# Rotary attention and a dense mixture of experts on one core: shorter rope tables, joined tail loads, a new order for the first batch's pairs, two subtractions moved to VectorE and four sums moved to GpSimd

## The chip, the cores and the metric

The kernel runs on one core of a Trainium2 chip. The metric is the device time of one execution in microseconds (us). Before the change it is 558.88 us, the median of three runs that lie between 558.83 and 558.90.

A core has five engines that run their own instruction streams and wait for each other on semaphores: TensorE (PE, matrix products; PEld is its loading of weights), VectorE (DVE), ScalarE (ACT), GpSimd (POOL) and SyncE (SP, which here only starts DMA transfers). [...]

## The reference

Attention with rotary embedding for q, k and v of shape 2 x 8 x 576 x 64, and a dense mixture of four experts over its output (1152 tokens of 512 values):

```python
def rotate(x):                       # cos, sin: 576 x 32, by position
    x1, x2 = x[..., :half], x[..., half:]
    return concat([x1 * cos - x2 * sin, x1 * sin + x2 * cos], -1)
scores = matmul(rotate(q), rotate(k).T) / sqrt(64)
attn = softmax(scores)               # exp(scores - max), over the sum + 1e-9
x = matmul(attn, v)                  # transposed to 1152 tokens x 512
p = domain_probs / (domain_probs.sum(-1) + 1e-9)
for e in range(4):                   # w1: 512 x 1024, w2: 1024 x 512
    h = maximum(x @ w1[e], 0)
    out += p[:, e:e+1] * (h @ w2[e])
```

## The kernel before

Most operands are split: a float32 value becomes a high part in the format fp32r and a low part, the difference between the value and its high part (`split`, L139 to L149). A product is then three matmuls: high by high, low by high, high by low. The high part is a copy, the low part a subtraction that reads two tiles from SBUF.

**First batch (0 to about 96 us).** Its eight heads are taken as four pairs (`Pair`). A pair's 576 positions are four blocks of 128 and a tail of 64; the tails of the pair's two heads share one block. Nine units `u` of work (four blocks for each head, then both tails) each go through: scores on PE (L365), row maximum on DVE (`max`, L376, tile `mx`), exponential on ACT (L387, tile `e`), transposes on PE (`turn_e`, L403, tile `pp`), a copy of these out of PSUM on DVE or ACT (`keep_e`, L430 to L437, tile `pt`), and the product with v (`values_of_four`, L446 to L455, one burst for each head). Then the division by the row sums, and the split of the pair's output into `xH` and `xL`, the operands of the experts: `xf`, 128x512, is the main part (`out_high` L562, `out_low` L566) and `xt`, 128x64, the tail (`tail_high` L587, `tail_low` L590 to L592). The low parts go to the engine that `spare_engine` (L594) names.

The order of issue is set by plan times: `place` (L597) puts each step of a unit on a heap (`Agenda`, L1036) at the pair's start plus the unit's number plus an entry of a table (`ALONE` for the first batch, `BESIDE` for the second), and the heap is emptied in the order of these numbers. The numbers are no times of the chip. One table serves all four pairs.

**Startup.** The rope tables come in one DMA on ACT's queue (L1138), laid out as `[128, 2, 5, 64]`: cosine, then sine with its sign, 64 values for each position, and ACT copies four blocks of each for the second head (L1145). q and k of a pair come in a DMA for the blocks (L181) and two of 64x64 for the tails, one for each head (L187). DVE rotates the first pair's k (L203, L207, L211, then its split), POOL its q and, behind that, q and k of the second pair; PE transposes them (`tpk`, `tpq`, L312).

**Second batch and first 512 tokens of the experts (about 96 to 343 us).** The experts' first layer (`ph`, L793 to L795), its split (`hH`, `hL`) and second layer (`po`, L768 to L770) run between the steps of the second batch's attention. The weights are split as they arrive: ACT copies the high part (L680, `wh`, 128x1024), POOL subtracts (L681, `wl`).

**Last 640 tokens (about 343 to 552 us).** `Moe1` computes the first layer with seven products over halves, for which `Weights.sum` (L692) forms four sums of weight blocks (`sf`, L701), then their split (`sh` on ACT, `sl` on POOL). For the first weight block of expert 0 the sums are POOL's, otherwise DVE's. DVE also adds the products up (L971) and makes `hL` (L982).

Of the kernel before, what the change touches and what calls it, by code (L numbers as in the profile page):

```python
# [22 lines left out]

ALONE = dict(
    scores=-0.216, max=-0.086, exp=0.449, turn_e=1.843, keep_e=1.923, turn_x=1.854, keep_x=2.839, values=3.902,
    keep_values=3.939, keep_values_2=4.037, tail_turn=1.866, copy_e=2.785, tail_turn_x=1.883, copy_x=2.045,
    inverse=1.86, spread=2.789, rows=3.299, divide=3.371, out_high=6.829, out_low=7.765, tail_rows=2.632,
    keep_tail_rows=3.895, tail_values=2.929, tail_divide=4.52, tail_high=4.659, tail_low=5.033,
)
BY_VECTOR = (0, 2)  # L30
BESIDE = dict(
# [4 lines left out]
    tail_low=2.554,  # L36
)

TURNS = [
    dict(  # L40
        k0=(5.275, 5.496), k1=(5.861, 6.017), q0=(7.136, 7.195), q1=(9.095, 9.116), k_tails=(5.379, 5.571),
        q_tails=(9.309, 9.652), swap=7.117,
    ),
    dict(
        k0=(3.155, 3.369), k1=(3.874, 3.89), q0=(6.063, 6.216), q1=(7.829, 8.028), tails=(5.059, 5.169),
        swap=5.239,
    ),
    dict(
        k0=(2.921, 3.395), k1=(4.09, 4.369), q0=(6.714, 6.914), q1=(7.075, 7.485), tails=(5.006, 5.12),
        swap=8.171,  # L50
    ),
]
# [10 lines left out]
def kernel(  # L63
# [75 lines left out]
    def split(eng_h, eng_l, src, hi, lo):  # L139
# [9 lines left out]
        eng_l.tensor_tensor(out=lo, in0=src, in1=f32(hi), op=ALU.subtract)  # L149


    class Pair:
# [12 lines left out]
        def load(self, s, queue=nc.sync, heads=((0, 2),)):  # L165
# [14 lines left out]
            for i, (a, z) in enumerate(heads):  # L180
                queue.dma_start(  # L181
                    out=x[:, a:z, 0:NR, :], in_=hs[a:z, 0:SM, :].rearrange("h (p r) d -> p h r d", r=NR)
                )
                if i:
                    continue
                for j in range(2):
                    queue.dma_start(out=x[j * ST : (j + 1) * ST, 0, NR, :], in_=hs[j, SM:S, :])  # L187
            self.raw[s] = x

        def rotate(self, which, eng, a=0, z=NC, pool=None):  # L190
# [11 lines left out]
            hl = self.hl[which][:, a:z]  # L202
            eng.tensor_tensor(out=t1, in0=x, in1=tabs[:, 0, a:z], op=ALU.mult)  # L203
            yield
            for lo, hi in ((0, D // 2), (D // 2, D)):
                o = D // 2 - lo
                eng.tensor_tensor(  # L207
                    out=t2[:, :, lo:hi], in0=x[:, :, o : o + D // 2], in1=tabs[:, 1, a:z, lo:hi], op=ALU.mult
                )
# [6 lines left out]
        def rotate_whole(self, which, eng):  # L216
# [6 lines left out]
            x = self.raw[which].rearrange("p h r d -> p (h r) d")[:, 0:NC]  # L223
            eng.tensor_tensor(out=t1, in0=x, in1=tabs[:, 0], op=ALU.mult)
            yield
            for lo, hi in ((0, D // 2), (D // 2, D)):
                o = D // 2 - lo
                eng.tensor_tensor(
                    out=t2[:, :, lo:hi], in0=x[:, :, o : o + D // 2], in1=tabs[:, 1, :, lo:hi], op=ALU.mult
                )  # L230
# [363 lines left out]
        def spare_engine(self):  # L594
            return nc.vector if (self.b, self.hp) == (B - 1, NP - 1) else nc.gpsimd

        def place(self, u, t, step, o):  # L597
# [8 lines left out]
            if u == TAIL:  # L606
                at("tail_turn", self.turn_e, u)
                at("tail_turn_x", self.turn_x, u)
                for key in (
                    "copy_e", "copy_x", "inverse", "spread", "rows", "divide", "out_high", "out_low", "tail_rows", "keep_tail_rows",  # L610
                    "tail_values", "tail_divide", "tail_high", "tail_low",
                ):
# [3 lines left out]
            if self.plain:
                at("keep_e", self.keep_e, u, nc.vector if u % NR in BY_VECTOR else nc.scalar)
                if u % 2:
                    at("turn_x", self.turn_x, u)
                    at("keep_x", self.keep_x, u)  # L620
                if u % NR == NR - 1:
                    j = u // NR
                    at("values", self.values_of_four, j)
                    at("keep_values", self.keep_values, j, 0, nc.vector)
                    at("keep_values_2", self.keep_values, j, 1, nc.scalar)
                return
            at("high", self.high, u)
# [7 lines left out]
    class Weights:  # L635
# [501 lines left out]
    apart = ((0, 1), (1, 2))  # L1137
    nc.scalar.dma_start(out=tabs[:, :, 0:NS], in_=rope)  # L1138
# [5 lines left out]
    for x in range(2):  # L1144
        nc.scalar.activation(out=tabs[:, x, NS:], in_=tabs[:, x, 0:NR], func=AF.Copy)  # L1145
    pr.rotate_now("k", nc.vector, 0, NS)
# [48 lines left out]
    for hp, pr in enumerate(first):  # L1195
        n = hp * U
        for u in range(U):
            pr.place(u, n + u, 1, ALONE)
        if hp + 1 < NP:
# [7 lines left out]
            plan.at(n + t["swap"], nx.swap)  # L1207
    load_qk(2.6, first[2])
    load_v(U + 5.8, first[2])
    load_qk(U + 0.05, first[3])  # L1210
    load_v(2 * U + 5.8, first[3])
    load_qk(2 * U + 0.4, second[0])
    load_v(3 * U + 9.3, second[0])
    for t in (6.5, 21.2, 30.2):
        plan.at(t, wts.load)
    for t in (30, 33):
        plan.at(t, later(wts.split))
    end = NP * U + 8.5
    for i in range(int(2 * end) - 1):
# [73 lines left out]
def _rope_tables(S, D):  # L1293
# [40 lines left out]
```

## Time and profile before

| | before |
|---|---|
| median of the runs | 558.88 us |
| profiled execution, its own time | 558.97 us |
| its span, first to last instruction | 557.2 us |
| PE busy, share of the span | 532.4 us, 96% |
| DVE | 317.5 us, 57% |
| ACT | 273.9 us, 49% |
| POOL | 318.3 us, 57% |
| mean granted TensorE clock, share of full speed | 0.998 |

The busy shares are means over stages that differ. PE is the only engine near its limit, so the time can be read as PE's busy time plus the stretches in which PE stands: 557.2 - 532.4 = 24.8 us, of which 4.7 us come after its last matmul. In a listing of waits, "A <- B" says that A's engine stood until B was done.

### The profile page before, as it was taken

What the parts mean: (1) busy time and instruction counts of PE and PEld (TensorE: products, weight loads), DVE (VectorE), ACT (ScalarE), POOL (GpSimd) and SP (SyncE); (2) the same over time, 40 slices, a digit from 0 to 9 for tenths busy, and PEclk for the clock granted to TensorE, in tenths of its full rate; (3) what the DMA queues carried; (4) which work ended last, traced back from release to release, by engine and by line L of the source; (5) the groups of instructions that cost most, each with busy time, mean ns of one, the idle gap of its engine ahead of it and who ended that gap; (6) DMA issues with size and microseconds to landing.
All of it is one profiled execution on the core that took longest, in us unless ns stands there. A gap on an engine that the chain in (4) does not pass through costs nothing.

```text
span 557.2 us, 8532 instructions
## 1 busy us (share of the span) xinstructions
PE 532.4 (96%) x3189; PEld 459.9 (83%) x3189; DVE 317.5 (57%) x605; ACT 273.9 (49%) x556; POOL 318.3 (57%) x238
## 2 busy tenths in 40 slices
PE   3899989999999999999999999999999999999996
PEld 2677777788888888888788878988998899889985
DVE  6578675444465435554365427894777477657602
ACT  4667666663565546564556554352443234315300
POOL 7999914659334933483453497478555653565400
PEclk9999999999999999999999999999999999999999
DMA  5525303453235222522252215431232223222102
GB/s 153 137 64 142 80 1 101 124 167 103 76 74 153 75 77 73 155 77 76 49 137 75 76 41 177 162 114 38 77 113 77 76 68 120 78 63 91 38 1 94
DMA packets 48731, 51.16 MB, mean 92 GB/s; under 512 B 15538, under 2 KB 38322, under 8 KB 48690
## 3 DMA queue, kind: packets, MB, share of 16 engines
q1 hardware_dynamic: 47890, 49.87, 30.3%
q10 hardware_dynamic: 800, 0.75, 0.5%
q8 instruction: 25, 0.41, 0.3%
q14 instruction: 16, 0.13, 0.1%
HBM read 43.34 MB, written 2.36 MB: 82 GB/s over the span
## 4 chain that ended last, share of the span: by engine, by line
PE 77%; ACT 7%; DVE 6%; POOL 5%; issue 1%; SPq 1%; DMA 1%; ACTq 0%; DVEq 0%; POOLq 0%
PE po L1030 6%; PE po L1029 6%; PE po L1028 6%; PE sc L365 6%; PE p L942 6%; PE p L940 6%; PE p L941 5%; PE ph L794 4%; PE ph L795 4%; PE po L770 4%; PE po L768 4%; PE ph L793 4%; PE po L769 4%; PE pp L403 4%; PE x L455 3%; ACT e L387 2%
## 5 line engine op out<-in xcount | busy, mean ns | idle before, releaser
L681 POOL TENSOR_TENSOR wl<-wr,wh 128x1024 fp32r<-128x1024 f32 x64 | 154.0, 2411 | 145.5 <-ACT wh L680 145.5
L680 ACT ACTIVATE wh<-wr 128x1024 fp32r<-128x1024 f32 x64 | 67.2, 1052 | 21.8 <-issue 11.0
L376 DVE TENSOR_REDUCE mx<-sc 128x1 f32<-128x576 f32 x72 | 54.3, 754 | 33.3 <-PE sc L365 31.3
L149 POOL TENSOR_TENSOR sl<-sf,sh 128x1024 fp32r<-128x1024 f32 x16 | 38.5, 2408 | 43.4 <-ACT sh L142 43.4
L387 ACT ACTIVATE e<-sc,mx 128x576 f32<-128x576 f32 x72 | 53.4, 742 | 19.2 <-DVE mx L376 18.9
L1030 PE MATMUL po<-wh,hL 128*128 128x512 f32 x160 | 62.3, 389 | 0.0
L1029 PE MATMUL po<-wl,hH 128*128 128x512 f32 x160 | 62.3, 389 | 0.0
L1028 PE MATMUL po<-wh,hH 128*128 128x512 f32 x160 | 62.3, 389 | 0.0
L768 PE MATMUL po<-wh,hH 128*128 128x512 f32 x128 | 51.6, 403 | 0.0
L793 PE MATMUL ph<-xH,wh 128*128 128x512 f32 x128 | 51.1, 399 | 0.0
L794 PE MATMUL ph<-xL,wh 128*128 128x512 f32 x128 | 50.1, 391 | 0.8 <-POOL xL L566 0.8
L795 PE MATMUL ph<-xH,wl 128*128 128x512 f32 x128 | 50.1, 392 | 0.0
L770 PE MATMUL po<-wh,hL 128*128 128x512 f32 x128 | 50.1, 392 | 0.0
L769 PE MATMUL po<-wl,hH 128*128 128x512 f32 x128 | 49.9, 390 | 0.0
L980 ACT ACTIVATE hH<-p 128x320 fp32r<-128x320 f32 x64 | 26.0, 435 | 38.8 <-DVE p L971 38.8
L403 PE MATMUL pp<-ident,e 128*128 128x128 f32 x288 | 43.8, 275 | 1.2 <-ACT e L387 0.8
L754 DVE SCALAR_TENSOR_TENSOR hL<-ph,hH 128x512 fp32r<-128x512 f32 x32 | 22.2, 692 | 39.8 <-ACT hH L753 39.6
L701 DVE TENSOR_TENSOR sf<-wr 128x256 f32<-128x256 f32 x30 | 33.1, 1141 | 17.0 <-DMA wr<-in_moe_w_dram 17.0
L142 ACT ACTIVATE sh<-sf 128x1024 fp32r<-128x1024 f32 x16 | 17.0, 1060 | 51.1 <-DVE sf L701 51.1
L403 PEld LDWEIGHTS pp<-ident,e 128*128 128x128 f32 x288 | 34.3, 140 | 7.6 <-ACT e L387 2.2
L982 DVE SCALAR_TENSOR_TENSOR hL<-p,hH 128x320 fp32r<-128x320 f32 x64 | 30.9, 486 | 14.8 <-ACT hH L980 14.5
L803 DVE SCALAR_TENSOR_TENSOR acc<-po,probs,acc 128x512 f32<-128x512 f32 x27 | 18.6, 748 | 33.0 <-PE po L1030 32.9
(221 smaller groups left out, 1307.8 us busy)
## 6 DMA issues: line engine op xcount, KB each, us to landing
wr<-in_moe_w_dram SPq DMA_DIRECT2D x68, 512.0 KB, 3.5
k2T<-kT SPq DMA_DIRECT2D x14, 320.0 KB, 4.4
rawv<-in_v_dram SPq DMA_DIRECT2D x16, 128.0 KB, 3.1
out_dram<-acc SPq DMA_DIRECT2D x8, 256.0 KB, 2.8
rawk<-in_k_dram SPq DMA_DIRECT2D x7, 256.0 KB, 3.8
rawq<-in_q_dram SPq DMA_DIRECT2D x7, 256.0 KB, 3.0
rawv<-in_v_dram SPq DMA_DIRECT2D x16, 32.0 KB, 2.3
tabs<-in_rope_dram ACTq DMA_DIRECT2D x1, 320.0 KB, 3.5
```

The costliest lines, as they stand in the source:

```text
L403: nc.tensor.transpose(pp[:, c * P : (c + 1) * P], self.e[u][:, c * P : (c + 1) * P], ident)
L680: nc.scalar.activation(out=wh, in_=raw, func=AF.Copy)
L681: low = lambda: nc.gpsimd.tensor_tensor(out=wl, in0=raw, in1=f32(wh), op=ALU.subtract)
L768: nc.tensor.matmul(po[t], lhsT=sH, rhs=wH, start=(f == 0), stop=False)
L769: nc.tensor.matmul(po[t], lhsT=sH, rhs=wL, start=False, stop=False)
L770: nc.tensor.matmul(po[t], lhsT=sL, rhs=wH, start=False, stop=(f == NF - 1))
L793: nc.tensor.matmul(o, lhsT=wH[:, kt], rhs=xh, start=(kt == 0), stop=False)
L794: nc.tensor.matmul(o, lhsT=wH[:, kt], rhs=xl, start=False, stop=False)
L795: nc.tensor.matmul(o, lhsT=wL[:, kt], rhs=xh, start=False, stop=(kt == KT1 - 1))
L1028: nc.tensor.matmul(po[t], lhsT=sH, rhs=wH, start=(f == 0), stop=False)
L1029: nc.tensor.matmul(po[t], lhsT=sH, rhs=wL, start=False, stop=False)
L1030: nc.tensor.matmul(po[t], lhsT=sL, rhs=wH, start=False, stop=(f == NF - 1))
```

## The change

It has seven parts.

1. The tables are 96 values for each position (cosine once, minus sine, sine) instead of 128. Cosine is broadcast over both halves (`times_cos`). The DMA is 128x480 values (240 KB) instead of 128x2x320 (320 KB), and ACT's copy is one of 128x384 instead of two of 128x256.
2. The two tail DMAs of each k and q load become one with a source of [2, 64, 64] and 128 partitions as its destination. At the start SP issues the second pair's k and q ahead of all v loads.
3. Three tables (`PAIRS`) replace `ALONE`: for the first pair, the two middle ones and the last; each unit has its own entries, and they also choose DVE or ACT for the copies.
4. The value burst is placed in three parts (blocks 0 and 1, 2 and 3, the rest).
5. `spare_engine` gives DVE the low parts of the last pair of both batches; before, that was so for the second batch alone.
6. In the second batch's last pair the four transposes of the tail's exponentials go ahead of the last group of value products (`BESIDE_VALUES`).
7. The four sums of the last weight block of expert 0 go to POOL, and their split is in two halves of 128x512. The sums are formed in the order 0, 1, 2, 3.

```diff
-    tabs = const.tile([P, 2, 2 * NR + 1, D], F32, name="tabs")
+    tabs = const.tile([P, NC, 3 * D // 2], F32, name="tabs")
...
+    def times_cos(eng, out, x, a, z):
+        cos = tabs[:, a:z, 0 : D // 2].unsqueeze(2).to_broadcast([P, z - a, 2, D // 2])
+        halves = (y.rearrange("p n (two d) -> p n two d", two=2) for y in (out, x))
+        eng.tensor_tensor(out=next(halves), in0=next(halves), in1=cos, op=ALU.mult)
...
-                for j in range(2):
-                    queue.dma_start(out=x[j * ST : (j + 1) * ST, 0, NR, :], in_=hs[j, SM:S, :])
+                queue.dma_start(out=x[:, 0, NR, :], in_=hs[:, SM:S, :])
...
-            eng.tensor_tensor(out=t1, in0=x, in1=tabs[:, 0, a:z], op=ALU.mult)
+            times_cos(eng, t1, x, a, z)
...
         def spare_engine(self):
-            return nc.vector if (self.b, self.hp) == (B - 1, NP - 1) else nc.gpsimd
+            return nc.vector if self.hp == NP - 1 else nc.gpsimd
...
+        def place_alone(self, u, n, o):
             def at(key, f, *args):
-                plan.at(t + step * o[key], lambda: f(*args))
+                plan.at(n + o[f"{key}{u}"], lambda: f(*args))
...
+                for key, chunks in (("values_a", (0, 2)), ("values_b", (2, 4)), ("values_c", (4, 5))):
+                    at(key, self.values_of_four, j, chunks)
...
+            ends = not e and fb in (0, NF // FB - 1)
             for o, p, q, op in (
-                (0, a21, a22, ALU.add), (2, a11, a21, ALU.subtract), (1, x[:, 0], a11, ALU.subtract),
+                (0, a21, a22, ALU.add), (1, x[:, 0], a11, ALU.subtract), (2, a11, a21, ALU.subtract),
                 (3, a12, x[:, 1], ALU.subtract),
             ):
-                (nc.vector if e or fb else nc.gpsimd).tensor_tensor(out=x[:, o], in0=p, in1=q, op=op)
+                (nc.gpsimd if ends else nc.vector).tensor_tensor(out=x[:, o], in0=p, in1=q, op=op)
...
-            if e or fb:
+            if ends and fb:
+                for i in (0, 2):
+                    split(nc.scalar, nc.gpsimd, *(y[:, i : i + 2] for y in (x, sh, sl)))
+            elif e or fb:
                 split(nc.scalar, nc.gpsimd, x, sh, sl)
...
-    pr.load("v")
-    for s in "kqv":
+    for s in "kq":
         nx.load(s)
+    for x in (pr, nx):
+        x.load("v")
...
-            pr.place(u, n + u, 1, ALONE)
+            pr.place_alone(u, n, PAIRS[0 if not hp else 2 if hp == NP - 1 else 1])
...
+            late = BESIDE_VALUES if hp == NP - 1 and u == TAIL - 1 else {}
+            pr.place(u, n + step * (u + 2), step, dict(when, **late))
```

Three places show what this does to the order. Line numbers are those of the respective kernel, and the numbers at the names' ends are instances.

The first is the end of the first batch's last pair (`xf_3`, `xt_3`) on POOL; `wl_0_0_2` and `wl_0_0_3` are the low parts of expert 0's next weight blocks, `vs` the split of the second batch's first v. Before:

```order
77 L144 TENSOR_SCALAR vs_0_1265<-rawv_0_1260 128x10x64
78 L149 TENSOR_TENSOR vs_0_1265<-rawv_0_1260,vs_0_1265 128x10x64
79 L592 TENSOR_TENSOR xL_76<-xt_3_1313,xH_74 128x64
80 L566 TENSOR_TENSOR xL_75<-xf_3_1215,xH_73 128x512
81 L681 TENSOR_TENSOR wl_0_0_2_1319<-wr_0_0_2_1141,wh_0_0_2_1318 128x1024
82 L681 TENSOR_TENSOR wl_0_0_3_1331<-wr_0_0_3_1316,wh_0_0_3_1330 128x1024
```

And after, first POOL, then DVE at the same place (`kT_0` belongs to the second batch's first pair):

```order
76 L635 TENSOR_TENSOR xL_75<-xf_2_956,xH_73 128x512
77 L204 TENSOR_SCALAR vs_0_1268<-rawv_0_1263 128x10x64
78 L209 TENSOR_TENSOR vs_0_1268<-rawv_0_1263,vs_0_1268 128x10x64
79 L767 TENSOR_TENSOR wl_0_0_2_1308<-wr_0_0_2_1126,wh_0_0_2_1307 128x1024
80 L767 TENSOR_TENSOR wl_0_0_3_1320<-wr_0_0_3_1305,wh_0_0_3_1319 128x1024
```

```order
115 L538 COPY xf_3_1204<-x_122 64x256
116 L629 TENSOR_TENSOR xf_3_1204<-xf_3_1204,pr_3_1296 128x512
117 L652 TENSOR_TENSOR xt_3_1302<-x_122,xt_3_1302 64x64 x2
118 L661 TENSOR_TENSOR xL_76<-xt_3_1302,xH_74 128x64
119 L635 TENSOR_TENSOR xL_75<-xf_3_1204,xH_73 128x512
120 L366 SCALAR_TENSOR_TENSOR kT_0_1329<-tpk_0_1322,kT_0_1329 64x512 x2
```

The two subtractions have left POOL, so its two `wl` follow `vs` directly, and stand on DVE between the divisions and `kT_0`. ACT's order there is unchanged: the copy `wh_0_0_2`, then `xH` from `xt_3`, `xH` from `xf_3`, then `wh_0_0_3`.

The second is the value burst of the first batch's second pair on PE (`x_122 <- pt_1_0`). Before, then after:

```order
83 L312 MATMUL tpq_2_695<-identr,hlq_20_370 128x128 x4
84 L365 MATMUL sc_1_7_705<-kT_1_380,qT_1_449 128x288 x2
85 L365 MATMUL sc_1_7_705<-k2T_1_441,qT_1_449 128x288 x2
86 L403 MATMUL pp_1_5_710<-ident,e_1_4_643 128x128 x4
87 L475 MATMUL x_121<-ident,e_1_4_643 128x128
88 L455 MATMUL x_122<-pt_1_0_548,rawv_1_158 64x256 x8
```

```order
83 L379 MATMUL tpq_2_686<-identr,hlq_20_363 128x128 x4
84 L524 MATMUL x_122<-pt_1_0_538,rawv_1_154 64x256 x4
85 L432 MATMUL sc_1_7_699<-kT_1_372,qT_1_442 128x288 x2
86 L432 MATMUL sc_1_7_699<-k2T_1_434,qT_1_442 128x288 x2
87 L470 MATMUL pp_1_5_704<-ident,e_1_4_629 128x128 x4
88 L544 MATMUL x_121<-ident,e_1_4_629 128x128
89 L524 MATMUL x_122<-pt_1_0_538,rawv_1_154 64x256 x4
```

Half of the rows of the burst's first product now stand ahead of the scores of unit 7. The third pair has the same exchange.

The third is DVE while the last 640 tokens go through the first hidden blocks of expert 0; `sf_3` are the four sums of part 7. Before:

```order
324 L982 SCALAR_TENSOR_TENSOR hL_0_1_3958<-p_3_3831,hH_0_1_3957 128x320
325 L701 TENSOR_TENSOR sf_3_3980<-wr_0_2_3_3796 128x256
326 L982 SCALAR_TENSOR_TENSOR hL_0_0_3888<-p_0_3970,hH_0_0_3887 128x320
327 L701 TENSOR_TENSOR sf_3_3980<-wr_0_2_3_3796 128x256
328 L701 TENSOR_TENSOR sf_3_3980<-sf_3_3980,wr_0_2_3_3796 128x256
329 L701 TENSOR_TENSOR sf_3_3980<-wr_0_2_3_3796,sf_3_3980 128x256
330 L971 TENSOR_TENSOR u_1_3999<-p_1_3992,p_0_1_3850 128x320
```

After, on POOL:

```order
178 L209 TENSOR_TENSOR sl_2_3912<-sf_2_3906,sh_2_3911 128x1024
179 L788 TENSOR_TENSOR sf_3_3963<-wr_0_2_3_3779 128x256
180 L788 TENSOR_TENSOR sf_3_3963<-sf_3_3963,wr_0_2_3_3779 128x256
181 L788 TENSOR_TENSOR sf_3_3963<-wr_0_2_3_3779 128x256
182 L788 TENSOR_TENSOR sf_3_3963<-wr_0_2_3_3779,sf_3_3963 128x256
183 L209 TENSOR_TENSOR sl_3_3970<-sf_3_3963,sh_3_3969 128x512 x2
```

The four sums now stand behind `sl_2` on POOL, and DVE goes from `hL_0_0` directly to `u_1`. For experts 1 to 3 they stay on DVE, with the second and third exchanged.

## Rows read from the trace of the kernel before

**Rows 1.** Waits of PE: what waited <- for what, total us, times, longest.

```profile
PE tlq L335 <- POOL xL L149: 1.4, 1, 1.4
...
PE tpq L312 <- POOL hlq L149: 0.9, 1, 0.9
PE ph L794 <- POOL xL L566: 0.8, 1, 0.8
...
PE x L507 <- DVE ptX L486: 0.7, 1, 0.7
PE p L940 <- DVE hL L982: 0.6, 1, 0.6
```

**Rows 2.** Timeline 96 to 104 us: start, duration, engine, line, [idle before].

```profile
96.35 1.06 ACT L680 ACTIVATE wh<-wr 128x1024 fp32r<-128x1024 f32 x1
97.32 0.24 ACT L588 ACTIVATE xH<-xt 128x64 fp32r<-128x64 f32 x1
...
97.99 1.04 ACT L680 ACTIVATE wh<-wr 128x1024 fp32r<-128x1024 f32 x1
98.16 1.27 POOL L566 TENSOR_TENSOR xL<-xf,xH 128x512 fp32r<-128x512 f32 x1 [0.20 <-ACT xH L563]
99.39 4.75 POOL L681 TENSOR_TENSOR wl<-wr,wh 128x1024 fp32r<-128x1024 f32 x2
...
99.48 0.50 PE L794 MATMUL ph<-xL,wh 128*128 128x512 f32 x1 [0.85 <-POOL xL L566]
```

**Rows 3.** Timeline 362 to 385 us, two-input subtractions on POOL and DVE.

```profile
370.67 7.32 POOL L681 TENSOR_TENSOR wl<-wr,wh 128x1024 fp32r<-128x1024 f32 x3 [1.65 <-ACT wh L680]
374.08 4.20 DVE L701 TENSOR_TENSOR sf<-wr 128x256 f32<-128x256 f32 x2
```

**Rows 4.** Stretches: length, PE, PEld, DVE, ACT, POOL busy, PEclk, DMA share, GB/s.

```profile
552.50:553.00 0.50, 0.02 (x1) 0.00 (x0) 0.50 (x2) 0.00 (x0) 0.00 (x0) 1.00 1.00 377
...
555.00:555.50 0.50, 0.00 (x0) 0.00 (x0) 0.00 (x0) 0.00 (x0) 0.00 (x0) 0.50 0.90 279
```

**Rows 5.** Timeline of PE, the first scores and the same form later.

```profile
11.57 0.81 PE L365 MATMUL sc<-kT,qT 128*128 128x288 f32 x2
...
16.27 0.49 PE L365 MATMUL sc<-kT,qT 128*128 128x288 f32 x2
```

**Rows 6.** DMA issues: target <- source, queue, count, KB each, us to landing.

```profile
tabs<-in_rope_dram ACTq DMA_DIRECT2D x1, 320.0 KB, 3.5
...
rawk<-in_k_dram SPq DMA_DIRECT2D x16, 16.0 KB, 3.1
```

**Rows 7.** Timeline of POOL at its first rotation and its last at startup.

```profile
4.88 0.45 POOL L203 TENSOR_TENSOR t1q<-rawq,tabs 128x128 f32<-128x128 f32 x1 [1.91 <-DMA rawq<-in_q_dram]
...
27.25 1.40 POOL L149 TENSOR_TENSOR hlq<-t1q,hlq 128x576 fp32r<-128x576 f32 x1
```

**Rows 8.** Page part 3, DMA queues: packets, MB, share of 16 engines' span.

```profile
q1 hardware_dynamic: 47890, 49.87, 30.3%
```

**Rows 9.** Timelines at 45 us and 80 to 82 us, PE and DVE.

```profile
45.29 0.54 PE L365 MATMUL sc<-kT,qT 128*128 128x288 f32 x2 [0.18 <-ACT e L387]
...
80.60 0.76 DVE L376 TENSOR_REDUCE mx<-sc 128x1 f32<-128x576 f32 x1
...
...
81.72 0.53 PE L365 MATMUL sc<-kT,qT 128*128 128x288 f32 x2 [1.40 <-ACT e L387]
```

**Rows 10.** Timeline of PE at 333 us, the tail's four transposes.

```profile
332.91 0.60 PE L403 MATMUL pp<-ident,e 128*128 128x128 f32 x4
```

**Rows 11.** Timelines at 344 us and 359 to 365 us, the sums and their split.

```profile
344.36 0.87 POOL L701 TENSOR_TENSOR sf<-wr,sf 128x256 f32<-128x256 f32 x1
...
359.79 0.41 DVE L701 TENSOR_TENSOR sf<-wr 128x256 f32<-128x256 f32 x1
...
361.31 0.42 DVE L701 TENSOR_TENSOR sf<-wr,sf 128x256 f32<-128x256 f32 x1
...
362.90 2.39 POOL L149 TENSOR_TENSOR sl<-sf,sh 128x1024 fp32r<-128x1024 f32 x1 [3.68 <-ACT sh L142]
```

More of the change, by code (lines that the diff above doesn't have):

```diff
@@ L31 @@
+LOADS = dict(
+    qk2=2.6, v2=14.8, qk3=9.579, v3=23.8, qk4=18.4, v4=37.283, w0=6.71, w1=21.2, w2=30.197, s0=30.015, s1=33.0,
+    s2=-5.5, s3=-1.276, s4=-0.1, s5=-0.09,
+)
+END = dict(
+    end=8.5, narrow=-6.1,
+)
 BESIDE = dict(
@@ L37 @@
 )
+BESIDE_LAST = dict(
+    scores=-0.004, max=0.03, exp=0.181, turn_e=0.973, high=1.077, low=1.115, turn_x=1.327, high_x=1.328,
+    low_x=1.329, values=2.085, lower=2.576, add=2.643, tail_turn=1.093, copy_e=1.225,
+    tail_turn_x=1.122, copy_x=1.44, inverse=0.243, spread=0.555, rows=2.195, divide=2.503,
+    out_high=2.55, out_low=2.6, tail_rows=2.032, keep_tail_rows=2.1, tail_values=2.033, tail_divide=2.527, tail_high=2.528,
+    tail_low=2.554,
+)
+BESIDE_OUT = dict(out_high=4.0, out_low=4.3)
+BESIDE_VALUES = dict(values=2.1, lower=2.58, add=2.643)
+BESIDE_LOADS = dict(qk=3.5, v=12.2)
 TURNS = [
     dict(
-        k0=(5.275, 5.496), k1=(5.861, 6.017), q0=(7.136, 7.195), q1=(9.095, 9.116), k_tails=(5.379, 5.571),
-        q_tails=(9.309, 9.652), swap=7.117,
+        k0=(5.275, 5.496), k1=(5.795, 6.017), q0=(7.136, 7.195), q1=(9.06, 9.081), k_tails=(5.379, 5.571),
+        q_tails=(9.309, 9.652), swap=7.072,
     ),
@@ L207, in rotate @@
                 eng.tensor_tensor(
-                    out=t2[:, :, lo:hi], in0=x[:, :, o : o + D // 2], in1=tabs[:, 1, a:z, lo:hi], op=ALU.mult
+                    out=t2[:, :, lo:hi], in0=x[:, :, o : o + D // 2], in1=sin(a, z, lo, hi), op=ALU.mult
                 )
@@ L223, in rotate_whole @@
             x = self.raw[which].rearrange("p h r d -> p (h r) d")[:, 0:NC]
-            eng.tensor_tensor(out=t1, in0=x, in1=tabs[:, 0], op=ALU.mult)
+            times_cos(eng, t1, x, 0, NC)
             yield
@@ L228, in rotate_whole @@
                 eng.tensor_tensor(
-                    out=t2[:, :, lo:hi], in0=x[:, :, o : o + D // 2], in1=tabs[:, 1, :, lo:hi], op=ALU.mult
+                    out=t2[:, :, lo:hi], in0=x[:, :, o : o + D // 2], in1=sin(0, NC, lo, hi), op=ALU.mult
                 )
@@ L608, in place @@
                 at("tail_turn_x", self.turn_x, u)
[L609 to L612, printed above, removed]
+                for key in self.ENDS:
                     at(key, getattr(self, key))
@@ L615, in place @@
             at("turn_e", self.turn_e, u)
[L616 to L626, printed above, removed]
             at("high", self.high, u)
@@ L1106, with pick @@
         pr.qTt = qTt[pr.pool is odds]
+    def pick(x):
+        return nc.vector if x > 0 else nc.scalar
     jobs = collections.deque()
@@ L1137 @@
     apart = ((0, 1), (1, 2))
-    nc.scalar.dma_start(out=tabs[:, :, 0:NS], in_=rope)
+    nc.scalar.dma_start(out=tabs[:, 0:NS], in_=rope)
     pr.load("k", heads=apart)
     pr.load("q", nc.scalar, apart)
-    pr.load("v")
-    for s in "kqv":
+    for s in "kq":
         nx.load(s)
-    for x in range(2):
-        nc.scalar.activation(out=tabs[:, x, NS:], in_=tabs[:, x, 0:NR], func=AF.Copy)
+    for x in (pr, nx):
+        x.load("v")
+    nc.scalar.activation(out=tabs[:, NS:], in_=tabs[:, 0:NR], func=AF.Copy)
     pr.rotate_now("k", nc.vector, 0, NS)
@@ L1207 @@
             plan.at(n + t["swap"], nx.swap)
[L1208 to L1214, printed above, removed]
+    load_qk(LOADS["qk2"], first[2])
+    load_v(LOADS["v2"], first[2])
+    load_qk(LOADS["qk3"], first[3])
+    load_v(LOADS["v3"], first[3])
+    load_qk(LOADS["qk4"], second[0])
+    load_v(LOADS["v4"], second[0])
+    for t in (LOADS["w0"], LOADS["w1"], LOADS["w2"]):
         plan.at(t, wts.load)
-    for t in (30, 33):
+    for t in (LOADS["s0"], LOADS["s1"]):
         plan.at(t, later(wts.split))
-    end = NP * U + 8.5
+    end = NP * U + END["end"]
     for i in range(int(2 * end) - 1):
@@ L1234, in start_experts @@
             plan.at(end + i, lambda: next(moe), lambda: work(2))
-    plan.at(end - 6, narrow)
+    plan.at(end + END["narrow"], narrow)
     plan.at(end, start_experts)
```

113 lines of the change are left out of this document (91 added, 22 removed).

## The prediction

> **What bounds the kernel now.** I read the busy shares first (PE 96%), then PE's waits, then a timeline around each wait that the change can touch. PE is the bound everywhere, so an edit counts only by what it does to a stretch in which PE stands. The waits that it touches are short: 1.4 us for POOL's `xL` and 0.9 us for its `hlq` at startup, 0.8 us for `xL` at the end of the first batch, 0.7 us for `ptX` in the second batch's last pair, 0.6 us for `hL` behind the sums [rows 1]. The list has no wait for the sums of experts 1 to 3, so their order on DVE costs or gives nothing. The reader is to see that all waits in reach sum to a few microseconds. A new wait of the length of one POOL subtraction (2.4 us) outweighs most of them together.
>
> **The low parts on DVE (part 5).** This is the term that decides. Before, PE stands until POOL's `xL <- xf` and starts again at 99.48 [rows 2]. POOL did that subtraction ahead of the two `wl`, which then ran back to back for 4.75 us. Now POOL has nothing in front of `wl_0_0_2`: its input, ACT's first `wh`, ends at 96.35 + 1.06 = 97.41, so it starts at about 97.5. DVE's first low part needs ACT's `xH <- xt`, which ends at 97.32 + 0.24 = 97.56 [rows 2]. POOL is ahead by about 0.1 us, and ACT's order makes it so.
>
> What a subtraction of two SBUF tiles does on DVE while POOL subtracts is in the trace: POOL ran three `wl` back to back from 370.67 to 377.99, and DVE's two sums, which take 0.41 each when alone [rows 11], took 4.20 us for the two, from 374.08 to 378.28 [rows 3]. With 7.32 / 3 = 2.44 us for one `wl`, POOL's second ended at 375.55 and its third at 377.99: the first sum got through between these two and the second waited for the third. So each of DVE's operations waits for the POOL operation that runs, and POOL's next one gets in ahead of DVE's next one. It ended 0.29 us after POOL did.
>
> The same pattern here: the tail's low part waits for `wl_0_0_2`, which ends at 97.5 + 2.38 = 99.88 (half of 4.75 each); `wl_0_0_3` has its input since 97.99 + 1.04 = 99.03, gets in, and ends at 102.25; the main low part (512 elements, so twice the 0.29) ends at 102.83, and PE starts at 102.88. That is 102.88 - 99.48 = **+3.4 us**. From below: if DVE were not held, its main low part would start at 98.16, where POOL's started, and end 0.7 us later (0.42 us for 256 elements, less than twice that for 512): PE at 98.9, -0.6 us. Behind the waiting subtractions on DVE stand `kT` and then `hL`; both follow PE's products, which are late by as much, so I add nothing for them. POOL's `wl` come 1.9 us earlier, which nobody waited for.
>
> **The clock behind that wait.** PE would stand from 98.63 (99.48 less its wait of 0.85) to 102.88, 4.2 us, while the longest of its waits in the pairs before was 1.40 [rows 9]. After its last matmul, which ends at 552.52, the granted clock reads 1.00 up to 553.0 and 0.50 from 555.0 [rows 4]. That is a fall from 2.4 to 1.2 GHz within 2.5 us without work, so I expect one in a stretch of 4.2. What it costs I take from the startup: there the same pair of score matmuls takes 0.81 us at 11.57 and 0.49 at 16.27 [rows 5]. Over the 4.7 us between the two rows that is 4.7 x (1 - 0.49 / 0.81) = **+1.9 us**. The bounds are 0 (the clock stays up) and twice that.
>
> **Startup (parts 1 and 2).** The way to PE's `tpq` at 28.7 us goes through POOL, which works without a pause from 4.88 to 28.65 [rows 7]; it starts when `rawq` and `tabs` are there. Landing hardly depends on size: 3.5 us for 320 KB, 3.1 for 16 KB [rows 6]. So 80 KB less give 0.4 x 80 / 304 = -0.1 us. Cosine by broadcast: no row shows it; the same counts of elements are read and written, so 0. The joined tail does away with issues that nobody waited for on SP, and its landing I leave where it is: the sum goes by **-0.1 us**. Bounds: -0.4 (the whole of that difference) and +1.5 (the joined tail lands later by half of a landing time, and POOL's q waits for it; DVE's k has 1.4 us to spare, since PE then waits for POOL [rows 1]).
>
> Here the Trainium skill speaks against the change. Its page "DMA: Bandwidth & Descriptors", section "Why a DMA increments its semaphore by 16 and not by 1", says that a DMA uses as many engines as divide the slowest dimension of source and destination; with the two heads outermost in the source these would be two instead of 16. An estimate by it with the mean packet of this trace (30.3% of 16 x 557 us over 47,890 packets, 56 ns [rows 8]) is 64 packets, 3.6 us, on either engine; no load of this shape has a landing time in the trace of before. By that rule the sum would be higher by what of the 3.6 us reaches POOL, 563.7 or more.
>
> **Bursts and the last pair's order (parts 3 and 4).** At 45.29 PE stood 0.18 us for an exponential [rows 9]. Eight matmuls of the burst now lie in front of it, so the wait goes; the third pair has the same one: **-0.35 us** (0 to -0.6). In the last pair PE stands 1.40 us at 81.72 [rows 9]: DVE's maximum of the unit before came at 80.60 and its exponential behind that. Now a copy moves from ACT to DVE ahead of that maximum, while ACT is freed of it: the wait moves rather than goes, **-0.1 us**, bounds ±0.4.
>
> **Transposes ahead of the values (part 6).** PE's 0.7 us for `ptX` [rows 1] are covered by four transposes of the tail (0.60 us with the drain of the last [rows 10], 0.44 to PE's next start): **-0.44 us** (0 to -0.67). They followed the values without a wait. If their exponential is not there 1.8 us earlier, the gain is 0.
>
> **Sums on POOL (part 7).** Four sums leave DVE, the first at 359.79, the last at 361.31, 4 x 0.42 = 1.67 us [rows 11]. They stand ahead of the `hL` for which PE waits 0.6 us [rows 1], and of ACT's and POOL's split, whose `sl` ends at 362.90 + 2.39 = 365.29. POOL stood 3.68 us before that `sl`, from 359.22 [rows 11]. Four sums at 0.87 there take 3.5 us, half of `sl` another 1.2: its first half is done at 363.9, 1.4 us sooner. So the gain lies between the 0.6 of the one wait and these 1.4, and I take the middle, **-1.0 us**; the bounds are 0 (PE waits for the second half, done at 365.1) and -1.4.
>
> **Sum.** 3.4 + 1.9 - 0.1 - 0.35 - 0.1 - 0.44 - 1.0 = +3.3, of which the parts that gain are -2.0. The profiled execution is 558.97, which gives 562.3; the median of the runs is 0.09 lower, so 562.2.
>
> **Rivals.**
> - *The wait without the clock* (the stall comes, the clock stays): 562.2 - 1.9 = 560.3. For it: no stretch of this length lies between busy ones in the trace, and the only fall shown is at the end.
> - *One wait instead of two.* DVE gets in first or its second subtraction slips in ahead of `wl_0_0_3`. Then the main low part waits for one `wl` only, which ends at about 100.1, and PE starts at about 100.75: +1.3, no fall of the clock: 562.2 - 1.9 - 2.1 = 558.2. For it: POOL's lead is 0.1 us. Against: ACT's order gives POOL the lead, and in rows 3 POOL did get in between.
> - *DVE is not held* (faster): all gaps close as meant, 558.9 - 0.6 - 2.0 = 556.3. Against it stands the 4.20 us of rows 3. It decides if DVE's two low parts take 1 us together.
> - *A late start* (slower by more): the q tails hold POOL's second rotation, +1.5 on top of the forecast: 563.7. For it: POOL has no pause up to 28.65 in which it could catch up [rows 7]. Against: its first rotation reads blocks only. The rule of the Trainium skill's page on DMA, above, would bring it about.
> - *The new order does nothing*: bursts, transposes and sums give none of their 1.9 us: 564.1.
>
> **How the numbers follow.** Forecast 0.40; the wait without the clock 0.20; one wait 0.17; not held 0.13; a late start or nothing from the order 0.10. About 0.2% (1.1 us) is what a measurement of this kernel can tell from no change, so faster is below 557.8 and slower above 560.0. Slower: nearly all of the forecast (0.38), over half of the second case (0.12), most of the last (0.09): 0.59. Faster: the case without holding, and a third of the one-wait case: 0.19. The rest is 0.22. The range goes from 557.0, which leaves out most of the not-held case, to 563.7, which leaves out a late start with everything else. The forecast's own range is 560.9 to 563.7.
>
> **What would show it.** In the profile after: DVE's `xL <- xf` at about 100 with over 2 us, ending 0.5 us behind a POOL `wl`, and PE's first L794 waiting about 4.2 us for DVE; a granted clock below 1.00 at 102 to 106 us; scores at 45 us without a wait; the transposes at about 331 in place of the 0.7 us; no wait for `hL` near 364; POOL's first rotation within 0.5 us of 4.88. The forecast is wrong if the low parts on DVE end before 100, or if PE's clock reads 1.00 through the stall.

## The result and the profile after

The changed kernel takes 563.03 us (median of four runs, 561.53 to 563.27) against 558.89 before: 1.0069 times the time, with a 95% interval of 1.0054 to 1.0084. The forecast was 562.2 in a range of 557.0 to 563.7. The profiled execution took 563.11 us with a span of 561.3; before, these were 558.97 and 557.2.

The waits of PE in the changed kernel, in the same columns as [rows 1]:

```profile
PE ph L884 <- DVE xL L635: 4.1, 1, 4.1
...
PE tlq L402 <- POOL xL L209: 2.2, 1, 2.2
...
PE tpq L379 <- POOL hlq L209: 0.7, 1, 0.7
```

The wait of `ph` for `xL` has grown from 0.8 to 4.1 us and has another releaser, DVE. The waits for `ptX` and for `hL` of [rows 1] are no longer there. The one for POOL's `xL` at startup is 0.8 longer.

The timeline of the changed kernel around the long wait, which answers to [rows 2]:

```profile
97.45 0.24 ACT L657 ACTIVATE xH<-xt 128x64 fp32r<-128x64 f32 x1
...
97.63 4.67 POOL L767 TENSOR_TENSOR wl<-wr,wh 128x1024 fp32r<-128x1024 f32 x2 [3.56 <-ACT wh L766]
...
97.73 2.35 DVE L661 TENSOR_TENSOR xL<-xt,xH 128x64 fp32r<-128x64 f32 x1 [0.65 <-ACT xH L657]
...
100.00 2.84 DVE L635 TENSOR_TENSOR xL<-xf,xH 128x512 fp32r<-128x512 f32 x1
...
102.90 0.80 PE L884 MATMUL ph<-xL,wh 128*128 128x512 f32 x1 [4.13 <-DVE xL L635]
...
104.35 0.63 PE L884 MATMUL ph<-xL,wh 128*128 128x512 f32 x1
...
108.10 0.39 PE L884 MATMUL ph<-xL,wh 128*128 128x512 f32 x1
```

POOL's two subtractions run from 97.63 to 102.30. DVE's first low part, of 64 elements, takes 2.35 us. Its second takes 2.84 and ends 0.54 us after POOL. Behind the stall PE's products stand 0.43 us apart and take 0.63; from 108 on they take 0.39 again. The stretches of the changed kernel say why (columns as in [rows 4]; the figure behind the busy times is the granted clock):

```profile
100.00:101.00 1.00, 0.00 (x0) 0.00 (x0) 1.00 (x2) 0.92 (x3) 1.00 (x1) 1.00 0.00 0
101.00:102.00 1.00, 0.00 (x0) 0.00 (x0) 1.00 (x1) 0.00 (x0) 1.00 (x1) 0.58 0.93 96
102.00:103.00 1.00, 0.10 (x1) 0.10 (x1) 0.97 (x2) 0.00 (x0) 0.29 (x1) 0.50 1.04 406
...
107.00:108.00 1.00, 1.00 (x4) 0.81 (x3) 0.00 (x0) 0.00 (x0) 0.00 (x0) 0.51 0.99 241
108.00:110.00 2.00, 2.00 (x12) 1.69 (x12) 0.60 (x1) 1.21 (x3) 0.00 (x0) 1.00 0.96 278
```

The clock falls from 2.4 to 1.2 GHz while PE stands and comes back at 108.

Where the 4.1 us of span went can be read by taking the same instruction in both timelines and noting by how much it is late:

| PE instruction | before, us | after, us | late | what lies in between |
|---|---|---|---|---|
| `tlq <- xL` | 11.41 | 12.06 | +0.65 | startup |
| `sc <- kT,qTt`, first pair | 29.07 | 29.70 | +0.63 | |
| `sc` of unit 7, last pair | 84.36 | 84.51 | +0.15 | pairs: -0.5 |
| first `ph <- xL` of the stall | 99.48 | 102.90 | +3.42 | the wait: +3.3 |
| twelfth product behind it | 102.11 | 107.76 | +5.65 | the clock: +2.2 |
| `x <- ident,e` behind the moved transposes | 333.35 | 338.38 | +5.03 | second batch: -0.6 |
| `p <- tH,sl` behind the sums | 365.35 | 369.63 | +4.28 | last tokens: -0.75 |
| end of the span | 557.2 | 561.3 | +4.1 | |

At startup POOL's rotations of q stand so in the changed kernel:

```profile
4.34 0.45 POOL L215 TENSOR_TENSOR t1q<-rawq,tabs 128x128 f32<-128x128 f32 x1 [1.37 <-DMA rawq<-in_q_dram]
...
8.58 0.67 POOL L215 TENSOR_TENSOR t1q<-rawq,tabs 128x192 f32<-128x192 f32 x1 [1.23 <-DMA rawq<-in_q_dram]
```

The first starts 0.54 us sooner than in [rows 7], but the second, which reads the joined tail, waits 1.23 us for a DMA.

The bursts, the last pair and the transposes in the changed kernel:

```profile
45.74 1.08 PE L524 MATMUL x<-pt,rawv 128*64 128x256 f32 x8
46.76 0.53 PE L432 MATMUL sc<-kT,qT 128*128 128x288 f32 x2
...
81.36 0.52 PE L432 MATMUL sc<-kT,qT 128*128 128x288 f32 x2
...
83.30 0.54 PE L432 MATMUL sc<-kT,qT 128*128 128x288 f32 x2 [1.04 <-ACT e L454]
...
336.48 0.60 PE L470 MATMUL pp<-ident,e 128*128 128x128 f32 x4
337.20 0.39 PE L576 MATMUL x<-pt,vs 128*128 128x256 f32 x1
```

Half a burst stands where PE waited 0.18 us [rows 9]. The last pair's 1.40 us at 81.72 is gone, but 0.58 stands at the score of the unit ahead of it (79.94) and 1.04 at that of the unit behind it; PE's waits for an exponential in this pair sum to 2.0 us in both kernels. The transposes fill the wait for `ptX`.

### The profile page after: what moved, and what is told of

The parts are those of the page before. It is cut to its first block, busy times and chain, and to the rows that moved or that the text cites. A ratio compares the mean times of both kernels' runs of the same rounds, so it can differ in the third digit from the quotient of the medians.

```text
span 561.3 us, 8508 instructions
## 1 busy us (share of the span) xinstructions
PE 534.6 (95%) x3189; PEld 461.3 (82%) x3189; DVE 319.4 (57%) x605; ACT 272.7 (49%) x554; POOL 320.2 (57%) x241
## 4 chain that ended last, share of the span: by engine, by line
PE 76%; DVE 8%; POOL 6%; ACT 6%; issue 2%; DMA 1%; ACTq 0%; POOLq 0%; DVEq 0%
PE sc L432 6%; PE po L1118 6%; PE po L1120 6%; PE po L1119 6%; PE p L1030 5%; PE p L1032 5%; PE p L1031 5%; PE ph L884 4%; PE po L860 4%; PE ph L885 4%; PE po L858 4%; PE po L859 4%; PE ph L883 4%; PE pp L470 4%; PE x L524 3%
## 5 line engine op out<-in xcount | busy, mean ns | idle before, releaser
L209 POOL TENSOR_TENSOR sl<-sf,sh 128x1024 fp32r<-128x1024 f32 (+1 forms) x17 | 38.7, 2279 | 39.5 <-ACT sh L202 39.5
L202 ACT ACTIVATE sh<-sf 128x1024 fp32r<-128x1024 f32 (+1 forms) x17 | 17.2, 1009 | 50.6 <-DVE sf L788 48.6
L432 PE MATMUL sc<-kT,qT 128*128 128x288 f32 x128 | 33.1, 340 | 4.2 <-ACT e L454 2.3
```

## The experiments

The theory: DVE's low parts are held by POOL's two `wl`, PE stands through it, and its clock falls. The rival: the loss comes from the rest, the joined tails and the new order above all. Each run was timed against the kernel before on the same chip; its time is the median.

**1. Low parts back on POOL.**

```diff
-            return nc.vector if self.hp == NP - 1 else nc.gpsimd
+            return nc.vector if (self.b, self.hp) == (B - 1, NP - 1) else nc.gpsimd
```

> The changed kernel with the last first-batch pair's two low parts back on GpSimd; all else as changed. Theory (VectorE is held by GpSimd's two weight subtractions, TensorE stands 4.1 us and its clock falls): the stall (+3.3) and the clock (+2.2) go, the gains of the bursts, the transposes and the sums (-1.9) and the late start (+0.6) stay: 563.0 - 5.5 = 557.5 us, granted clock 1.00 through 100 to 110 us. Rival (the loss comes from the joined tails and the new order of the pairs, the low parts add little): 561 to 563 us.

Measured: 557.52 us (before 558.93), ratio 0.9972 (0.9961 to 0.9983). The theory holds; that it does so to the tenth is luck, since the start alone varies by more from profile to profile (run 6). The timeline of this run:

```profile
97.88 1.27 POOL L635 TENSOR_TENSOR xL<-xf,xH 128x512 fp32r<-128x512 f32 x1 [0.20 <-ACT xH L632]
...
99.12 4.75 POOL L767 TENSOR_TENSOR wl<-wr,wh 128x1024 fp32r<-128x1024 f32 x2
99.21 0.50 PE L884 MATMUL ph<-xL,wh 128*128 128x512 f32 x1 [0.85 <-POOL xL L635]
```

It is the picture of [rows 2] again, with a wait of 0.85 us, and this one line turns a loss of 4.1 us into a gain of 1.4. The granted clock is 1.00 in every microsecond from 100 to 110.

**2. The low parts alone on DVE, in the kernel before.**

```diff
-            return nc.vector if (self.b, self.hp) == (B - 1, NP - 1) else nc.gpsimd
+            return nc.vector if self.hp == NP - 1 else nc.gpsimd
```

> The kernel before with this one edit: the low parts of the last first-batch pair on VectorE. Theory: + 3.3 us of stall and + 2.2 us of clock: 564.4 us; without the fall of the clock 562.2. Rival (the low parts add little by themselves): 559 to 560 us.

Measured: 563.57 us (before 558.93), ratio 1.0087 (1.0073 to 1.0101). One line costs 4.6 us. Its timeline and stretches:

```profile
97.50 4.66 POOL L681 TENSOR_TENSOR wl<-wr,wh 128x1024 fp32r<-128x1024 f32 x2 [4.87 <-ACT wh L680]
97.60 2.35 DVE L592 TENSOR_TENSOR xL<-xt,xH 128x64 fp32r<-128x64 f32 x1 [0.65 <-ACT xH L588]
...
99.88 2.84 DVE L566 TENSOR_TENSOR xL<-xf,xH 128x512 fp32r<-128x512 f32 x1
...
102.77 0.66 PE L794 MATMUL ph<-xL,wh 128*128 128x512 f32 x1 [4.12 <-DVE xL L566]
```

```profile
102.00:103.00 1.00, 0.23 (x1) 0.23 (x2) 0.97 (x2) 0.00 (x0) 0.17 (x1) 0.97 1.01 393
103.00:104.00 1.00, 1.00 (x3) 0.80 (x3) 0.99 (x2) 0.11 (x1) 0.00 (x0) 0.50 0.04 14
...
106.00:107.00 1.00, 1.00 (x5) 0.77 (x5) 0.00 (x0) 0.00 (x0) 0.00 (x0) 0.82 1.17 210
107.00:108.00 1.00, 1.00 (x8) 0.82 (x7) 0.00 (x0) 0.13 (x1) 0.00 (x0) 1.00 0.76 230
```

The wait is the same (102.77 against 99.48, 3.3 us). Here the clock was low only from about 102.9 to 106.4, against 101.2 to 108.0 in the changed kernel's profile. The twelfth product behind the stall is 4.87 us late (106.98 against 102.11), so the clock cost 1.6 us in this profile instead of 2.2. In both that is 0.44 us for each microsecond that PE worked at the lower clock (3.6 and 5.1 us). The price of the clock is not fixed.

**3. The weight copy behind the low parts' inputs.** The low parts stay on DVE; ACT's `wh_0_0_2` is issued behind `xH` from `xt_3` and `xf_3`.

```diff
-    for t, u in ((LOADS["s2"], LOADS["s3"]), (LOADS["s4"], LOADS["s5"])):
-        plan.at(end + t, lambda: wts.next(True))
+    for t, at, u in ((LOADS["s2"], -2.6, LOADS["s3"]), (LOADS["s4"], LOADS["s4"], LOADS["s5"])):
+        plan.at(end + t, wts.load)
+        plan.at(end + at, lambda: wts.split(True))
         plan.at(end + u, wts.finish_split)
```

> The changed kernel, low parts still on VectorE, but ScalarE's copy of expert 0's third weight block is issued behind its two copies of the pair's output instead of ahead of them (its load stays where it is). GpSimd's subtraction then starts at about 99, when VectorE's low parts are done (about 98.6). Theory (the cost is the meeting of the two engines, not VectorE as such): VectorE takes under 1 us for both low parts, TensorE hardly stands: 563.0 - 4.1 - 2.2 = 556.7 us. Rival (VectorE's place in the order is the cost, the low parts being late there in any case): 560 us or more.

Measured: 557.77 us (before 558.93), ratio 0.9977 (0.9968 to 0.9987). The mechanism is as expected, the gain 1.1 us smaller:

```profile
96.63 0.23 DVE L661 TENSOR_TENSOR xL<-xt,xH 128x64 fp32r<-128x64 f32 x1 [0.32 <-ACT xH L657]
...
97.15 0.69 DVE L635 TENSOR_TENSOR xL<-xf,xH 128x512 fp32r<-128x512 f32 x1 [0.29 <-ACT xH L632]
...
98.15 4.73 POOL L767 TENSOR_TENSOR wl<-wr,wh 128x1024 fp32r<-128x1024 f32 x2 [6.08 <-ACT wh L766]
...
103.00 0.74 PE L342 MATMUL tpq<-ident,rotq 128*128 128x128 f32 x5 [1.62 <-DVE kT L366]
```

The same two subtractions take 0.23 and 0.69 us when POOL is idle, against 2.35 and 2.84 beside it. So the cost is the meeting, not the engine. But PE, now early, waits 1.62 us for DVE's `kT`, whose ACT part stood behind the two weight copies.

**4. PE kept at work through the wait.** The first expert product is issued 17 times more, each overwritten by the next; the extra ones compute nothing that is used.

```diff
+                    for _ in range(17 if (self.c, e, f, kt) == (0, 0, 0, 0) else 0):
+                        nc.tensor.matmul(o, lhsT=wH[:, kt], rhs=xh, start=True, stop=True)
```

> The changed kernel with TensorE's first expert product issued 17 times more, each time overwritten by the next, ahead of the stall: 17 x 0.23 = 3.9 us of useless work that ends where the low part is awaited. The stall itself stays as long, but TensorE works through most of it. Theory (the 2.2 us behind the stall are the clock): granted clock 1.00 through 100 to 110 us and 563.0 - 2.2 = 560.8 us. Rival (what is lost behind the stall is VectorE's and ScalarE's lateness): 563 us as before, products behind the stall still at 0.43 us each.

Measured: 560.30 us (before 558.93), ratio 1.0027 (1.0017 to 1.0037), 2.7 us less than the changed kernel although PE does 3.9 us of useless work:

```profile
102.21 0.50 PE L886 MATMUL ph<-xL,wh 128*128 128x512 f32 x1 [0.59 <-DVE xL L635]
102.55 0.40 PE L887 MATMUL ph<-xH,wl 128*128 128x512 f32 x1
```

```profile
101.00:102.00 1.00, 0.62 (x3) 0.19 (x1) 1.00 (x1) 0.00 (x0) 0.61 (x1) 1.00 0.88 342
102.00:103.00 1.00, 0.79 (x3) 0.67 (x4) 0.95 (x3) 0.01 (x1) 0.00 (x0) 1.00 0.39 150
103.00:104.00 1.00, 1.00 (x6) 0.80 (x5) 0.95 (x3) 0.59 (x1) 0.00 (x0) 1.00 0.00 0
```

The products behind the wait take 0.40 us at once and the clock reads 1.00. So the 2.2 us behind the stall are the clock and not late operands. The other 0.5 us are the start: this profile is 0.77 us earlier at `tlq` (11.29 against 12.06), with the same instructions up to there.

**5. The second batch's k ahead of both weight copies.** As run 3, but `wts.split` comes behind `kT` for both blocks:

```diff
-    for t, u in ((LOADS["s2"], LOADS["s3"]), (LOADS["s4"], LOADS["s5"])):
-        plan.at(end + t, lambda: wts.next(True))
-        plan.at(end + u, wts.finish_split)
+    for t, u in ((LOADS["s2"], -0.07), (LOADS["s4"], -0.06)):
+        plan.at(end + t, wts.load)
+        plan.at(end + u, wts.split)
```

> As the run with the weight copy behind, but both of ScalarE's next weight copies stand behind its copies of the second batch's k as well (loads unchanged). There TensorE stood 1.62 us at 103 for VectorE's part of that k, which waited for ScalarE's, which had stood behind the two weight copies. Theory (that wait was what ate the gain): it goes, 557.8 - 1.6 = 556.2 us. Rival (TensorE then waits for the copies of the hidden blocks or for the weights' low parts instead): 557.3 us or more.

Measured: 559.31 us (before 558.94), ratio 1.0008 (0.9999 to 1.0016). The theory fails: 3.1 us more than it said, and the rival was right. The wait at 103 went, and others came, in this run's timeline:

```profile
102.78 0.37 SPq L747 DMA_DIRECT2D wr<-in_moe_w_dram  x1
...
108.93 1.06 ACT L766 ACTIVATE wh<-wr 128x1024 fp32r<-128x1024 f32 x1 [3.33 <-DMA wr<-in_moe_w_dram]
...
111.23 0.49 PE L432 MATMUL sc<-k2T,qT 128*128 128x288 f32 x2 [0.57 <-DMA k2T<-kT]
...
116.14 0.65 PE L470 MATMUL pp<-ident,e 128*128 128x128 f32 x4 [1.69 <-ACT e L454]
```

The `wl` started at 100.35 instead of 99.12 (run 1). A weight buffer is free only when its `wl` is done, so the next load was issued at 102.78 instead of 101.54. ACT then stood 3.33 us for it and 1.81 for the one after it, with the copies of the hidden blocks queued behind. DVE's maximum stood behind the low part of such a block, and PE stood 1.69 us at 116 for the exponential that needs this maximum. This chain is read from one profile; run 11, where the load is issued at 100.47, has 0.53 us in place of the 1.69.

**6. The joined tails alone, in the kernel before.**

```diff
-                for j in range(2):
-                    queue.dma_start(out=x[j * ST : (j + 1) * ST, 0, NR, :], in_=hs[j, SM:S, :])
+                queue.dma_start(out=x[:, 0, NR, :], in_=hs[:, SM:S, :])
```

> The kernel before with one edit: the two tail loads of each k and q joined into one with two heads outermost in its source. Theory (a joined tail lands later; in the profile of the changed kernel GpSimd's second rotation waited 1.23 us for it): 558.9 + 0.3 to 0.7 = 559.2 to 559.6 us. Rival (fewer issues let the other loads start earlier, the landing is the same): 558.4 to 558.8.

Measured: 559.35 us (559.12 to 559.98; before 558.94), ratio 1.0005 (0.9997 to 1.0014). The median is 0.4 higher, as the theory had it, but the interval holds 1. In its profile PE's first transposes come at 9.47 instead of 8.20, for DVE's k, and `tlq` at 12.22 instead of 11.41. ACT's DMA queue carries the first q and its tail; here it is before and then in this run, in the columns of [rows 8]:

```profile
q10 hardware_dynamic: 800, 0.75, 0.5%
...
q10 hardware_dynamic: 770, 0.75, 0.4%
```

The same bytes come in 30 packets fewer. In the first 9 us the trace counts 80 packets of 4 bytes on this queue before, for five loads, and 50 here, for four: where each of the others has 16, the joined one has 2. It also ends later. From 6.7 to 9 us this queue moves 7 to 60 packets in the six profiles with joined tails, and none in the eight with two loads. With the shorter tables and the new order of the loads, `tlq` starts at 11.55 on average with joined tails (11.14 to 12.06, five profiles) and at 11.01 with two (10.80 to 11.15, runs 8, 9 and 11). So the profiles show a cost of about 0.5 us at the start, which the times of this run alone could not tell from nothing.

**7. The sums alone, in the kernel before.** Their old order is kept.

```diff
-                (nc.vector if e or fb else nc.gpsimd).tensor_tensor(out=x[:, o], in0=p, in1=q, op=op)
+                (nc.gpsimd if ends else nc.vector).tensor_tensor(out=x[:, o], in0=p, in1=q, op=op)
...
+            if ends and fb:
+                for i in (0, 2):
+                    split(nc.scalar, nc.gpsimd, *(y[:, i : i + 2] for y in (x, sh, sl)))
```

> The kernel before with one edit: the four sums of expert 0's last weight block on GpSimd and their split in two halves; the order of the sums as before. Theory (VectorE's sums stood in front of the hidden block and the split): TensorE's wait at 364 goes, 558.9 - 1.0 = 557.9 us. Rival (GpSimd's slower sums move the wait to the second half of the split): 558.5 to 559.2.

Measured: 557.68 us (before 558.94), ratio 0.9974 (0.9963 to 0.9984): -1.26, a little more than the theory. On POOL the four sums of this run took 0.72 to 0.75 us each, not 0.87 as in [rows 11], and the split ends at 364.73 instead of 365.29.

**8. Run 5 with two tail loads again** (the reverse of the edit of run 6).

> The run with k first, and the tails again as two loads for each k and q; short tables and the order of the loads as in the changed kernel. Theory (the joined tails cost 0.3 to 0.7 us at the start): 556.2 - 0.5 = 555.7 us. Rival (the start is set by the tables and the blocks): 556.2.

Measured: 559.41 us (558.62 to 561.31; before 558.94), ratio 1.0013 (1.0003 to 1.0022); run 5 took 559.31. No difference, but both scatter by about 2 us, so the times tell nothing of the tails; the 555.7 us also rested on run 5's 556.2, which had failed. In this run the scatter goes with the clock: seven executions with a mean granted clock of 0.998 or more took 558.6 to 559.5 us, five with 0.995 or 0.996 took 560.3 to 561.3.

**9. Run 1 with two tail loads again.**

> The changed kernel with the low parts back on GpSimd and the tails again as two loads for each k and q. Theory (the joined tails cost 0.3 to 0.6 us at the start; bursts, transposes and sums gain 1.9): 557.5 - 0.4 = 557.1 us. Rival (at the start the shorter tables and the new order of the loads matter, the tails do not): 557.5.

Measured: 557.06 us (556.75 to 557.18; before 559.07 on its chip), ratio 0.9962 (0.9948 to 0.9975), the fastest version here: 2.0 us under before, where run 1 was 1.4 under. The intervals overlap; in its profile POOL's second rotation does not wait and `tlq` starts at 11.09 instead of 11.72.

**10. The shorter tables alone, in the kernel before.** The edit is the one of the tables in the change: tile, DMA, copy and `times_cos`.

```diff
-            eng.tensor_tensor(out=t1, in0=x, in1=tabs[:, 0, a:z], op=ALU.mult)
+            times_cos(eng, t1, x, a, z)
```

> The kernel before with the shorter rope tables alone (cosine by broadcast, one table copy). Theory (a landing hardly depends on its size, and the broadcast costs nothing): 558.9 - 0.1 = 558.8 us. Rivals: the rotations start 0.5 us sooner, 558.4; or reading by broadcast makes GpSimd slower, 559.4 or more.

Measured: 558.85 us (before 559.07), ratio 0.9994 (0.9985 to 1.0003). A gain of over 0.9 us and a loss of over 0.2 are out, and with that the slower rotations; between the theory's -0.1 and the other rival's -0.5 it can't tell.

**11. The k between the two weight copies**, two tail loads, low parts on DVE. The diff is that of run 5 with -2.6 in place of its -0.07, -0.07 in place of its -0.06, and the tails as in run 9.

> The changed kernel, low parts on VectorE, two tail loads; ScalarE's order: both copies of the pair's output, the first weight copy, the second batch's k, the second weight copy. Theory (with k first the weights' low parts came 1.2 us late, so the next weight load was issued late and its copy made TensorE stand at 115; with both weight copies first the k was late; this order gives each its time): TensorE waits under 0.7 us for k, the weight load is issued no later than 103, 556.4 to 556.8 us. Rival (VectorE's low parts gain nothing in any order, since what is saved is waited for within 15 us): 557.3 or more.

Measured: 557.08 us (before 559.07), ratio 0.9965 (0.9953 to 0.9978). PE is 0.92 us ahead of run 9 behind the low parts, at 97.78:

```profile
101.94 0.74 PE L343 MATMUL tpq<-ident,rotq 128*128 128x128 f32 x5 [0.67 <-DVE kT L367]
```

It loses most of it here, and it is 0.15 us behind run 9 at 115. So it is as fast as run 9 and no faster, and the truth lies between theory and rival: the order can undo the loss on DVE, but what DVE saves over POOL is waited for a little later.

**12. Sums and moved transposes, in the kernel before.** Run 7 and, for the last unit before the tail of the second batch's last pair:

```diff
+            late = dict(values=2.1, lower=2.58, add=2.643) if hp == NP - 1 and u == TAIL - 1 else {}
```

> The kernel before with two edits: expert 0's last four sums on GpSimd (alone 1.26 us faster) and the four transposes of the tail ahead of the last value products of the second batch. Theory (the transposes fill a wait of 0.67 us): 557.7 - 0.4 = 557.3 us, and no wait for ptX in the list. Rival (the values wait for something else as long, or the exponential is not there yet): 557.7.

Measured: 557.62 us (before 559.12), ratio 0.9972 (0.9961 to 0.9982). Run 7 was 1.26 under its before, this is 1.50: no difference that can be told. The wait for `ptX` is gone from the list, but in this run's profile PE stands a little later for DVE:

```profile
331.94 0.60 PE L403 MATMUL pp<-ident,e 128*128 128x128 f32 x4
...
360.12 0.42 PE L944 MATMUL p<-tH,sh 128*128 128x320 f32 x1 [0.46 <-DVE hL L986]
```

In this profile the 0.5 us gained at 333 are lost at 360, and the timed runs show no more of them. The profile is the slowest of the run's eight executions (558.56 us), and it shows something else: behind the last pair's wait of 1.39 us at 81.70, which the kernel before has too, the granted clock reads 0.72 in 80 to 85 us and 0.94 in 85 to 90.

## Why the prediction was right

- **The low parts.** Forecast +3.4 us, measured +3.3 (99.48 to 102.90, less what came from ahead). POOL was first by 0.10 us, its second `wl` got in between DVE's two, and DVE ended 0.54 us behind POOL (estimate 0.58). The two rivals that rested here, one wait only and no holding, are out. The Trainium skill's page "SBUF — State Buffer", section "SBUF: two separate sides", says that a DVE operation with two SBUF inputs and a GpSimd operation that reads SBUF exclude each other for whole instructions. Runs 2 and 3 agree: 0.23 and 0.69 us alone, 2.35 and 2.84 beside `wl`.
- **The clock.** Forecast +1.9, measured +2.2 in the profile and 1.6 in run 2's. Run 4 shows that it is the clock. That the size is so close is in part luck: the forecast took 0.40 us for each of 4.7 us from two startup rows, at both of which the granted clock reads 1.00, so they do not show the clock's price; measured were 0.44 us for each of 5.1. The rival in which the clock stays up is out, though the shortest run of the changed kernel, 561.53 us at a mean clock of 0.997 instead of 0.992 to 0.994, seems to have paid less for it (it has no trace).
- **Startup.** This is the step that failed: forecast -0.1, measured +0.65. POOL did start 0.54 us sooner, and then lost 1.23 at the q tail. The prediction had left the joined tail's landing where it was because size hardly matters, and kept +1.5 as a bound. What its sum left out is the shape of the load: the joined tail has 2 packets of 4 bytes where the other loads have 16, its queue ends later, and it costs about 0.5 us at the start (run 6). What the prediction drew from the Trainium skill's page "DMA: Bandwidth & Descriptors", section "Why a DMA increments its semaphore by 16 and not by 1", points the same way: two engines instead of 16 for a load with the two heads outermost. The counts of 2 and 16 agree with it, though the trace names no engine for a packet. Of the 3.6 us estimated by it, POOL's second rotation waited for 1.23 in the changed kernel's profile, 0.92 in run 1, 0.19 in run 5 and nothing in runs 3, 4 and 6.
- **Bursts and last pair.** Forecast -0.45 together, measured -0.48 in the profile: -0.33 up to the last pair's first score (70.26 before, 70.56 after) and -0.15 from there to its unit 7, where the waits moved and did not go. Not run by themselves.
- **Transposes.** Forecast -0.44; in the profile -0.5 at the place. Run 12 could not find it in the time.
- **Sums.** Forecast -1.0; -0.75 between 333 and 365 in the profile, -1.26 alone (run 7).

The total came out 0.8 us above the forecast, and the startup's 0.75 is nearly all of that; the other differences, +0.33 for the clock and +0.25 for the sums the largest, cancel. The two large terms, 5.3 us forecast and 5.5 measured, carried it.

## What to carry to other kernels

Before moving a two-input SBUF operation to an idle DVE, look at what POOL does at that moment: an engine that is idle in the busy shares can still be held, and here back-to-back POOL work held each of a pair of DVE operations once. Price a new PE wait of several microseconds with the clock behind it. Before joining small loads into one, ask what the joined shape does to the landing; equal bytes and one issue less do not make it free. When an order is changed to start one engine's work later, follow the buffer that this work frees to the load that waits for it.

## What the runs showed that was not expected

- Freeing a weight buffer 1.2 us later (run 5) went with a time 3.1 us above the expectation and 1.5 above run 3: the next load was issued 1.2 us later, and ACT stood for it with other copies queued behind.
- The time that the clock stays low behind a stall of the same length differs from run to run: about 101.2 to 108.0 us in one profile, 102.9 to 106.4 in another. And a wait of 1.39 us can already have a low clock behind it (run 12's profile, 82 to 86 us), where the same wait of 1.40 us in the profile of before had none.
- The start of the kernel is not the same in each execution: with the same joined loads, POOL's second rotation waited 1.23 us in one profile, 0.92 in that of run 1, and not at all in that of run 3.
